# Softmax normalisation of 24 of 32 head groups on GpSimd instead of VectorE, with a new static order

## The chip, the cores and the metric

The kernel runs on one core of a Trainium2 chip. The metric is the device time of one launch in microseconds (us); lower is better. The engines are named as in the profile: PE (TensorE, matmuls), DVE (VectorE), ACT (ScalarE), POOL (GpSimd), SP (SyncE, which issues the DMAs).

## The reference

Two layers, each an attention block and an MLP block with a residual, on x of 2048 tokens by 640 in float32. The attention is local and dilated: each token looks at itself and at the seven tokens 2, 4, ... 14 before it; 32 heads of 20.

```python
def _A_ref(x, wqkv, wo):
    H = 32; Dh = D // H
    W, dil = 8, 2
    qkv = (x @ wqkv).reshape(B, S, 3, H, Dh)
    idx = pos[:, None] - (jnp.arange(W) * dil)[None, :]
    ...
    logits = jnp.einsum("bhsd,bhswd->bhsw", q, kg) * scale
    logits = jnp.where(mask, logits, -1e9)
    attn = softmax(logits, axis=-1)
    o = jnp.einsum("bhsw,bhswd->bhsd", attn, vg)
    return o.reshape(B, S, D) @ wo

def _B_ref(x, w1, b1, w2, b2):
    h = gelu(layernorm(x) @ w1 + b1)      # 640 -> 1536
    return h @ w2 + b2                    # 1536 -> 640

x = x + _A_ref(layernorm(x));  x = x + _B_ref(layernorm(x))
x = x + _A_ref(layernorm(x));  x = x + _B_ref(layernorm(x))
```

## The kernel before

The tokens are cut into four *units* of 512 (even and odd tokens apart, each in two halves), and with two layers there are eight unit passes n = 0 to 7; units 0 to 3 are layer one. In a unit each of 128 partitions holds four tokens. Every matrix product is computed in float16 in three passes over high and low halves, so each float32 operand is split first: ACT writes the high half, DVE the low one (L615 for normalised tokens, L435 for weights, L858 and L1076 for the MLP's hidden values).

A unit goes through these steps. Layernorm (for units 0 and 1 statistics by DVE, L561 to L563, and a power of -0.5 of one element on POOL, L566; for the others ACT sums and a power of two or one elements on POOL, L590). Products with wqkv on PE (L654; L661 for the very first tile, which is cut in three parts so that it can begin before the low halves are there), drained by ACT and spilled to DRAM. Then attention in four *head groups* of eight heads, G = 4n + g, all of it elementwise work: q times the eight windows of k (L741), the sum over the 20 channels that makes the logits (L745), for half of the units a mask (L750), maximum and difference (L753, L754), exp on ACT (L756), sum, reciprocal and product that normalise (L758, L759, L760), the product with v (L767) and three additions over the window (L775, L779). In units 0 to 2 a group's L741, L745 and L767 come in two halves of 2560 elements, from unit 3 on whole, 5120. The output is split (high half ACT, low half L788, on POOL for g = 0 to 2 and on DVE for g = 3), transposed by DMA (L799), multiplied by wo on PE (L810, eight blocks of fifteen matmuls in a unit) and added to x by DVE from PSUM (L816). Then the second layernorm and the MLP: first product L847, second L866 and L869, residuals L889; batches 5 to 7 go through a fast scheme with fewer columns (L1061 or L1024 for the first product, L1124 for the second, residuals L1143). POOL also adds the bias b2 to x (L624).

Nothing of this is scheduled by the hardware's own choice: every step is recorded with its needs, and three tables written into the file replay a schedule that a planner made earlier. ORDER lists all steps in the order in which they are issued, and so the order on each engine, which each works through in turn; PLACES gives the buffer of each tile; BESIDE names pairs, where the first step (on POOL) is given a wait for the second (on DVE), so that it begins with the DVE instruction that follows that one. In the kernel before, BESIDE ties 49 steps of L624 and L788 so. The attention's buffers set limits on the order: one for q and k, one for v, two for the products (both taken by a whole group), two for logits (`sm`).

At the start nine steps of eight matmuls on an identity (`warm`, L1153) keep PE busy until the first products; the normalised tokens of the first two tiles are transposed on PE (L489) and copied out by ACT (L497).

Of the kernel before, what the change touches and what calls it, by code (L numbers as in the profile page):

```python
# [261 lines left out]
def sliding_dilated_then_mlp_kernel(  # L262
# [87 lines left out]
    wo = sb.tile([P, 2, KD, D], HT, name="wo")  # L350
    b1 = sb.tile([P, NF], FT, name="b1")
    b2 = sb.tile([P, D], FT, name="b2")
    half = sb.tile([P, M], FT, name="half")
    junk = sb.tile([P, D], HT, name="junk")
    ident = sb.tile([P, P], HT, name="ident")
    bn = sb.tile([P, M, 14], FT, name="bn")
# [349 lines left out]
    def attention(G):  # L706
# [22 lines left out]
        def lgt():  # L729
            return lg().rearrange("p t w h -> p t h w")  # L730
# [428 lines left out]
    for _ in range(WARM):  # L1159
        warm([("sq", ("a", 0), 0)])  # L1160
# [74 lines left out]
```

## Time and profile before

| | |
|---|---|
| median of 3 runs | 1144.4 us (1144.36 to 1145.14) |
| the profiled execution's own time | 1144.26 us |
| its span in the trace | 1142.5 us |
| busy: PE, DVE, ACT, POOL | 1134.2, 1073.7, 552.5, 159.1 us |
| mean granted clock of PE | 0.998 |

The span runs from the first to the last instruction that the profiler shows; the execution's own time has 1.8 us around it. "Busy" is time in which at least one instruction of the engine runs. A group's row gives the source line, engine, operation, tiles written and read, shapes, how often, then busy time, mean duration in ns, and idle time before it with what ended that. PE's matmuls are pipelined, so a group's busy time divided by its count, and not its mean duration, is the pitch from one matmul to the next.

### The profile page before, as it was taken

Reading aid. Unit: us, or ns where it says so; the run is one execution under the profiler, and the core shown is the slowest. Engines: PE = TensorE matmul, PEld = TensorE weight load, DVE = VectorE, ACT = ScalarE, POOL = GpSimd, SP = SyncE. Lnnn points to the kernel's source line nnn. Section 1 sums busy time; section 2 is a strip of 40 time slices with the busy share of each in tenths; the row PEclk is TensorE's granted clock in tenths of the full one; section 3 lists DMA queues with packets and bytes.
Section 4 is the critical chain, followed back from the end, with each engine's and each line's share of the span. In section 5 each row is a group of like instructions: output and inputs, shape, how many; then the busy total and the mean of one; then the engine's idle time right before and its main releaser. Section 6 shows DMA issues by size and latency. Waiting matters only on the chain.

```text
span 1142.5 us, 17648 instructions
## 1 busy us (share of the span) xinstructions
PE 1134.2 (99%) x6932; PEld 647.0 (57%) x6932; DVE 1073.7 (94%) x1003; ACT 552.5 (48%) x977; POOL 159.1 (14%) x98
## 2 busy tenths in 40 slices
PE   8999999999999999999999999999999999999998
PEld 5444446577654565445555654556455546566886
DVE  8899999999999999999999999999999999988482
ACT  5476434545364438423645552355447542286360
POOL 2011110311111113100213011121211200300000
PEclk9999999999999999999999999999999999999999
DMA  9999999899976675956475866674598877788856
GB/s 295 324 311 277 278 331 279 262 266 308 240 198 196 216 192 125 253 182 188 155 216 188 179 188 188 213 190 133 164 267 275 258 209 221 211 218 225 251 152 189
DMA packets 259023, 257.38 MB, mean 225 GB/s; under 512 B 138540, under 2 KB 209532, under 8 KB 258940
## 3 DMA queue, kind: packets, MB, share of 16 engines
q1 hardware_dynamic: 258940, 256.26, 78.0%
q8 instruction: 54, 0.88, 0.3%
q14 instruction: 29, 0.24, 0.1%
HBM read 175.64 MB, written 48.71 MB: 196 GB/s over the span
## 4 chain that ended last, share of the span: by engine, by line
PE 99%; DVE 0%; DMA 0%; issue 0%
PE ps L654 34%; PE ps L847 17%; PE acc L866 14%; PE ps L810 11%; PE acc L1124 9%; PE ps L1061 7%; PE acc L869 4%; PE acc L1024 3%; PE ps L1024 1%; PE acc L1153 0%; DMA xf<-in_A_x_dram 0%; PE ps L661 0%; DVE bn L561 0%; PE acc L489 0%; DVE hl L615 0%; DVE bn L562 0%
## 5 line engine op out<-in xcount | busy, mean ns | idle before, releaser
L654 PE MATMUL ps<-wq,yT 128*128 128x480 f16 x1905 | 390.4, 366 | 0.0
L654 PEld LDWEIGHTS <-yT 128*128 128x128 f16 x1905 | 185.6, 98 | 197.0
L847 PE MATMUL ps<-yT,c 128*128 128x512 f16 (+1 forms) x1080 | 204.0, 344 | 0.0
L866 PE MATMUL acc<-c,act 128*128 128x512 f16 x720 | 203.4, 379 | 0.0
L741 DVE TENSOR_TENSOR pr<-qk 128x2560 f32<-128x2560 f32 (+1 forms) x44 | 179.6, 4088 | 0.7
L767 DVE TENSOR_TENSOR pr<-sm,v 128x2560 f32<-128x2560 f32 (+1 forms) x44 | 177.1, 4032 | 0.4
L745 DVE TENSOR_REDUCE sm<-pr 128x128 f32<-128x2560 f32 (+1 forms) x44 | 176.6, 4017 | 0.0
L847 PEld LDWEIGHTS <-c 128*128 128x128 f16 x1080 | 103.8, 98 | 87.4
L673 ACT ACTIVATE ev<-ps 128x480 f32<-128x480 f32 x128 | 70.7, 564 | 162.9 <-PE ps L654 155.5
L869 PE MATMUL acc<-c,act 128*128 128x128 f16 x720 | 148.2, 219 | 0.0
L775 DVE TENSOR_TENSOR pr<-pr 128x2560 f32<-128x2560 f32 (+2 forms) x88 | 143.8, 1645 | 0.2
L810 PE MATMUL ps<-wo,yT 128*128 128x320 f16 x960 | 134.7, 299 | 0.0
L866 PEld LDWEIGHTS <-act 128*128 128x128 f16 x720 | 70.3, 98 | 80.3 <-DVE act L858 0.2
L810 PEld LDWEIGHTS <-yT 128*128 128x128 f16 x960 | 93.0, 98 | 38.1
L590 POOL TENSOR_TENSOR ln<-ln,half 128x2 f32<-128x2 f32 (+1 forms) x30 | 48.6, 1621 | 408.9 <-ACT ln L587 408.9
L1124 PE MATMUL acc<-c,wq 128*128 128x320 f16 x630 | 92.9, 299 | 0.0
L853 ACT ACTIVATE act<-ps,b 128x512 f32<-128x512 f32 (+1 forms) x72 | 43.8, 613 | 93.1 <-PE ps L847 56.0
L624 POOL TENSOR_TENSOR xf<-xf,b 128x640 f32<-128x640 f32 x28 | 58.1, 2085 | 172.9 <-DVE xf L816 36.0
L788 POOL TENSOR_TENSOR ohl<-o,ohl 128x640 f16<-128x640 f32 x24 | 44.3, 1846 | 266.6 <-ACT ohl L786 118.7
L1061 PE MATMUL ps<-yT,c 128*128 128x512 f16 x360 | 78.7, 379 | 0.0
L1124 PEld LDWEIGHTS <-wq 128*128 128x128 f16 x630 | 61.6, 98 | 24.2
L571 ACT ACTIVATE junk<-xf 128x640 f16<-128x640 f32 x56 | 41.1, 733 | 66.8 <-DVE xf L816 54.8
(137 smaller groups left out, 1145.1 us busy)
## 6 DMA issues: line engine op xcount, KB each, us to landing
c<-mw SPq DMA_DIRECT2D x180, 320.0 KB, 4.0
spill<-ev SPq DMA_DIRECT2D x64, 480.0 KB, 5.6
qk<-spill SPq DMA_DIRECT2D x32, 880.0 KB, 5.4
v<-spill SPq DMA_DIRECT2D x32, 880.0 KB, 5.7
c<-msp SPq DMA_DIRECT2D x36, 320.0 KB, 3.6
qk<-spill SPq DMA_DIRECT2D x32, 320.0 KB, 4.8
c<-mw SPq DMA_DIRECT2D x54, 160.0 KB, 3.1
mw<-c SPq DMA_DIRECT2D x24, 320.0 KB, 5.6
```

What stands on the lines that cost most here:

```text
L654: nc.tensor.matmul(ps, transposed(yk)[:, a * KD + k, t * P:(t + 1) * P], wq[:, b, k, g], start=j == 0, stop=j == 3 * KD - 1)
L673: act(3 * GC, -400 + n, lambda i=i, pk=pk, ek=ek: nc.scalar.activation(tile_of(*ek)[:, :, i], tile_of(*pk)[:, :3 * GC].rearrange("p (a c) ...
L741: return nc.vector.tensor_mul(pr(pk), w[:, HALO + m + t0:HALO + m + t0 + TH, None, :].to_broadcast([P, TH, W, GC]), windows(w, t0, [GC, W] ...
L745: dve(E, G - 0.7, lambda pk=pk, t0=t0: nc.vector.tensor_reduce(lg(t0, t0 + TH).rearrange("p t w h -> p (t w h)"), pr(pk).rearrange("p t w ...
L767: return nc.vector.tensor_mul(pr(vk).rearrange("p t w (h d) -> p t (w h) d", d=DH), lg(t0, t0 + TH).rearrange("p t w h -> p t (w h)")[:, : ...
L775: dve(TH * w * GC, G - 0.9, lambda vk=vk, w=w: nc.vector.tensor_add(pr(vk)[:, :, 0:w], pr(vk)[:, :, 0:w], pr(vk)[:, :, w:2 * w]), need=[la ...
L810: nc.tensor.matmul(tile_of(*pk)[:, :D // 2], transposed(yk)[:, a * KD + k, t * P:(t + 1) * P], wo[:, b, k, c * D // 2:(c + 1) * D // 2], s ...
L847: nc.tensor.matmul(tile_of(*pk)[:, :nt], tile_of(*ck)[:, a, k * P:(k + 1) * P], transposed(yk)[:, c * KD + k, t0 * P:t1 * P], start=i == 0 ...
L866: nc.tensor.matmul(acc[i], w, tile_of(*wk)[:, c, :BANK], start=e == 0 and (a, c) == PASS[0], stop=end, skip_group_check=True)
L869: nc.tensor.matmul(acc[4][:, i * P:(i + 1) * P], w, tile_of(*wk)[:, c, BANK:], start=e == 0 and i == t0 and (a, c) == PASS[0], stop=end, s ...
L1061: nc.tensor.matmul(tile_of(*pk), tile_of(*ck)[:, a, k * P:(k + 1) * P], transposed(yk)[:, c * KD + k, :], start=i == 0, stop=i == 3 * KD - 1)
L1124: nc.tensor.matmul(acc[bank][:, :HD], tile_of(*hk)[half][:, a, slot, t * P:(t + 1) * P], load()[:, z, c], start=q in FIRST and i == 0 and ...
```

## The change

For the 24 groups with g = 0 to 2 the three DVE steps L758, L759 and L760 go. In their place POOL adds the exponentials in a tree (4, 2 and 1 window positions by eight heads by four tokens: 128, 64 and 32 elements), raises the 32 sums to the power of -1 and multiplies the 256 exponentials by the result; each of the five needs the one before. Each is tied by BESIDE so that the chain begins with the sum of logits (L745, now L760) of the next group. The groups with g = 3 stay as they were. A constant `minus` and a scratch tile `parts` are added; all groups share `parts`. The second token tile of the first products is cut in three parts too (`t in (0, 1)`), and the warming matmuls lose a need that only the planner used. The three tables are new throughout. Lines of the changed kernel lie some 14 to 31 further down.

```diff
@@ tables (all lines of ORDER and PLACES differ; of BESIDE the first) @@
-    278: 298, 302: 649, 326: 163, 395: 403, 400: 538, 405: 555, 410: 724, 497: 203, 520: 533, 543: 552, 607: 778, 612: 778, 617: 802, 622: 802,
+    269: 1, 270: 1, 271: 1, 272: 1, 273: 106, 283: 660, 295: 132, 296: 132, 297: 132, 298: 132, 299: 132, 309: 156, 321: 148, 322: 148, 323: 148,
@@ -351,6 +363,8 @@
     b1 = sb.tile([P, NF], FT, name="b1")
     b2 = sb.tile([P, D], FT, name="b2")
     half = sb.tile([P, M], FT, name="half")
+    minus = sb.tile([P, 1, 1], FT, name="minus")
+    parts = sb.tile([P, M * GH * W // 2], FT, name="parts")
     junk = sb.tile([P, D], HT, name="junk")
     ident = sb.tile([P, P], HT, name="ident")
     bn = sb.tile([P, M, 14], FT, name="bn")
@@ -394,6 +408,7 @@
         return nc.vector.memset(half, -0.5)
 
     dve(8, -900, constants, give=["half"])
+    dve(8, -100, lambda: nc.vector.memset(minus, -1.0), give=["minus"])
 
     def mask_index():
         nc.gpsimd.iota(mask, pattern=[[1, M], [1, W]], base=-HALO, channel_multiplier=M, allow_small_or_imprecise_dtypes=True)
@@ -655,7 +670,7 @@
                                              start=j == 0, stop=j == 3 * KD - 1)
                             j += 1
 
-                if n == 0 and g == 0 and t == 0:
+                if n == 0 and g == 0 and t in (0, 1):
                     def part(a, b, t=t, g=g, pk=pk):
                         for k in range(KD):
                             nc.tensor.matmul(tile_of(*pk)[:, :3 * GC], transposed(yk)[:, a * KD + k, t * P:(t + 1) * P], wq[:, b, k, g],
@@ -665,8 +680,8 @@
                     for a, c in ((0, 0), (1, 0), (0, 1)):
                         here = [("yT", ("a", n), t, a)] + [(("wq", "wqh")[1 - c], g, i) for i in range(3)]
                         mm(KD * 3 * GC, 5, -500, lambda a=a, c=c, part=part: part(a, c), need=here + last,
-                           give=[("qkvp", n, t, g) if c else ("qkvq", a)], use=[pk, yk])
-                        last = [("qkvq", a)]
+                           give=[("qkvp", n, t, g) if c else ("qkvq", t, a)], use=[pk, yk])
+                        last = [("qkvq", t, a)]
                 else:
                   mm(3 * KD * 3 * GC, 15, (-500 + n if n != NU else 24 + 11 * b) + 0.01 * k, product,
                    need=([("yT", ("a", n), t, a) for a in range(2)] if n == 0 and t not in (2, 3) else [("yT", ("a", n), t)]) + [("wq", g, i) for i in range(3)], give=[("qkvp", n, t, g)], use=[pk, yk])
@@ -755,10 +770,26 @@
             need=[("mx", G)], give=[("sub", G)], use=[sk])
         act(L, -450 + G, lambda: nc.scalar.activation(tile_of(*sk)[:, :L], tile_of(*sk)[:, :L], AF.Exp, scale=scale),
             need=[("sub", G)], give=[("e", G)], use=[sk], table="exp")
-        dve(L, G - 0.8, lambda: nc.vector.tensor_reduce(mx(1), lgt(), axis=AX.X, op=OP.add), need=[("e", G)], give=[("s", G)], use=[sk], more=0.19)
-        dve(8 * m * GH // 2, G - 0.8, lambda: nc.vector.reciprocal(mx(1), mx(1)), need=[("s", G)], give=[("rc", G)], use=[sk])
-        dve(L, G - 0.8, lambda: nc.vector.tensor_mul(lg(), lg(), mx(1)[:, :, None, :].to_broadcast([P, m, W, GH])),
-            need=[("rc", G)], give=[("at", G)], use=[sk])
+        if G in range(3, 32, 4):
+            dve(L, G - 0.8, lambda: nc.vector.tensor_reduce(mx(1), lgt(), axis=AX.X, op=OP.add), need=[("e", G)], give=[("s", G)], use=[sk], more=0.19)
+            dve(8 * m * GH // 2, G - 0.8, lambda: nc.vector.reciprocal(mx(1), mx(1)), need=[("s", G)], give=[("rc", G)], use=[sk])
+            dve(L, G - 0.8, lambda: nc.vector.tensor_mul(lg(), lg(), mx(1)[:, :, None, :].to_broadcast([P, m, W, GH])),
+                need=[("rc", G)], give=[("at", G)], use=[sk])
+        else:
+            after = ("lg", G + 1, 0 if (n + (g == NG - 1)) in WHOLE else m // EH - 1)
+            last = [("e", G)] + [("s", i) for i in range(G) if i not in range(3, 32, 4)][-1:]
+            for w in (4, 2, 1):
+                def add(w=w):
+                    part = parts.rearrange("p (t w h) -> p t w h", t=m, w=W // 2)
+                    src = lg() if w == W // 2 else part
+                    return nc.gpsimd.tensor_tensor(mx(1)[:, :, None, :] if w == 1 else part[:, :, :w], src[:, :, :w], src[:, :, w:2 * w], op=OP.add)
+
+                laid(m * w * GH, -700 + G, add, lambda ready, when, k=after: k in when, need=last, give=[("s", G) if w == 1 else ("sp", G, w)], use=[sk])
+                last = [("s", G) if w == 1 else ("sp", G, w)]
+            laid(m * GH, -700 + G, lambda: nc.gpsimd.tensor_tensor(mx(1), mx(1), minus.to_broadcast([P, m, GH]), op=OP.pow),
+                 lambda ready, when, k=after: k in when, need=[*last, "minus"], give=[("rc", G)], use=[sk])
+            laid(L, -700 + G, lambda: nc.gpsimd.tensor_tensor(lg(), lg(), mx(1)[:, :, None, :].to_broadcast([P, m, W, GH]), op=OP.mult),
+                 lambda ready, when, k=after: k in when, need=[("rc", G)], give=[("at", G)], use=[sk])
         for a in range(NE):
             t0 = a * TH
             vk = products(a, 1)
@@ -1157,7 +1188,7 @@
     load_x(0, -1000)
     prep_q(0, -990)
     for _ in range(WARM):
-        warm([("sq", ("a", 0), 0)])
+        warm([])
     layernorm(0, -500, ("yT", ("a", 0)), False)
     for g in range(1, NG):
         prep_q(g, -480 + g)
```

**DVE and POOL at group 2** (unit 0, halves of 2560). In both kernels `sm_85` holds the logits of group 2 here and `sm_86` those of group 3. DVE before, from the second product of q and k of group 3 to the products with v of group 2:

```order
L741 TENSOR_TENSOR pr<-qk_68 128x2560
L758 TENSOR_REDUCE sm_85<-sm_85 128x32
L745 TENSOR_REDUCE sm_86<-pr 128x128
L435 SCALAR_TENSOR_TENSOR c_77<-act,c_77 128x640
L745 TENSOR_REDUCE sm_86<-pr 128x128
L759 RECIPROCAL sm_85<-sm_85 128x32
L615 TENSOR_TENSOR hl_83<-y_80,hl_83 128x640
L760 TENSOR_TENSOR sm_85<-sm_85 128x256
L435 SCALAR_TENSOR_TENSOR c_79<-act,c_79 128x640
L767 TENSOR_TENSOR pr<-sm_85,v_69 128x2560 x2
```

DVE after, the same stretch:

```order
L756 TENSOR_TENSOR pr<-qk_68 128x2560 x2
L768 TENSOR_REDUCE sm_85<-sm_85 128x32
L769 TENSOR_TENSOR sm_85<-sm_85 128x256
L450 SCALAR_TENSOR_TENSOR c_77<-act,c_77 128x640
L760 TENSOR_REDUCE sm_86<-pr 128x128
L450 SCALAR_TENSOR_TENSOR c_78<-act,c_78 128x640
L760 TENSOR_REDUCE sm_86<-pr 128x128
L798 TENSOR_TENSOR pr<-sm_85,v_69 128x2560 x2
```

POOL after, beside it, between the low halves of groups 1 and 2:

```order
L819 TENSOR_TENSOR ohl_73<-o_84,ohl_73 128x4x160
L785 TENSOR_TENSOR parts<-sm_85 128x128
L785 TENSOR_TENSOR parts<-parts 128x4x16
L785 TENSOR_TENSOR sm_85<-parts 128x32
L789 TENSOR_TENSOR sm_85<-sm_85,minus 128x32
L791 TENSOR_TENSOR sm_85<-sm_85 128x256
L819 TENSOR_TENSOR ohl_73<-o_84,ohl_73 128x4x160
```

The normalisation of group 2 left DVE; POOL's five steps are tied to the L450 on c_78, and between that and the product with v that needs them stands one L760 of 2560 elements. Before, POOL had only L788 and L590 steps in this stretch.

**SP before the last unit's transposes.** The transposes L799 (now L830) of unit 7 feed its L810; the loads of L1055 (now L1086) bring the blocks of w1 for the first product of batch 6 (L1061). Before:

```order
L1055 DMA c_74<-mw_110 128x1280
L1055 DMA c_76<-mw_116 128x1280
L940 DMA v_69<-in_B_w_dram 128x5x128
L1055 DMA c_75<-mw_111 128x1280
L1112 DMA c_77<-mw_130 128x2x320
L940 DMA v_69<-in_B_w_dram 128x5x128
L1055 DMA c_74<-mw_117 128x1280
L940 DMA pr<-in_B_w_dram 128x5x128 x3
L1055 DMA c_76<-mw_112 128x1280
L799 DMA_TRANSPOSE yT_72<-ohl_73 128x10x128
L940 DMA pr<-in_B_w_dram 128x5x128
L799 DMA_TRANSPOSE yT_72<-ohl_73 128x10x128 x3
```

After:

```order
L1143 DMA c_74<-mw_133 128x2x320
L1143 DMA c_74<-mw_132 128x2x320
L1086 DMA c_76<-mw_116 128x1280
L971 DMA v_69<-in_B_w_dram 128x5x128 x2
L971 DMA pr<-in_B_w_dram 128x5x128 x3
L830 DMA_TRANSPOSE yT_72<-ohl_73 128x10x128 x3
L1086 DMA c_74<-mw_111 128x1280
L830 DMA_TRANSPOSE yT_72<-ohl_73 128x10x128
L1086 DMA c_75<-mw_110 128x1280
```

On PE nine of the twelve blocks of that first product stood ahead of the first L810 of unit 7, and one does now; one L810 block of unit 7 stands ahead of the one that was first.

**ACT at the start.** `wq<-pr` are the high halves of the first weight blocks, `yT<-acc` the copies of the first two tiles' transposes. Before:

```order
L613 ACTIVATE hl_82<-y_80 128x640
L434 ACTIVATE wq<-pr 128x5x160 x3
L613 ACTIVATE hl_82<-y_80 128x640
L613 ACTIVATE hl_83<-y_81 128x640
L497 ACTIVATE yT_70<-acc_94 128x5x128
L497 ACTIVATE yT_70<-acc_95 128x5x128
```

After:

```order
L628 ACTIVATE hl_82<-y_80 128x640
L449 ACTIVATE wq<-pr 128x5x160 x2
L512 ACTIVATE yT_70<-acc_94 128x5x128
L628 ACTIVATE hl_83<-y_81 128x640
L628 ACTIVATE hl_82<-y_80 128x640
L449 ACTIVATE wq<-pr 128x5x160
L512 ACTIVATE yT_70<-acc_95 128x5x128
```

The third weight block comes later on ACT, as its load does on SP, where a block of the second head group now stands between the second and the third. On PE all nine warming steps stand ahead of the first transposes, where four did.

More of the change, by code (lines that the diff above doesn't have):

```diff
@@ L71 @@
 ORDER = """
[111 rows of a table removed]
[113 rows of a table added]
 """
 PLACES = """
-000000000110000110101032320001111220230203102102132000110303222011120003200121102220011202120002200001001000110100001011000001110010221012110201100111
-010110011012022101012122011201022001001000001100010010010000011001020120120002110100121210001102101202010121202111002200000100100001100100001100001101
-000102112021120011001010100011011212000121202000200112000010010000011010000100100001101012020101220011001102011101001211202021210101021210201000100100
-000110100001001000011010210201210002110001100011001102201102001222010101221020001001000001101000010010000110100012200121000111100111111000020011202120
@@ L190 @@
-101022100011200010010000011010000100100001101011220021000101111002010110011021210100220112001211201000100100000110100001001000011010220010221200212301
-132012012112000002021102002111002021102002111102020102012111002021102012111000002021102002111102020102012111002021102002111102000102112111100000020201
-020121100020211020022111010201020122111010201020022101000000101010201221100101110200221110102010201221210101010201211200000002011102002112102010102012
-112002011102112112002001102202110100000020101222120100010111222020101010101222120100010111222020001102210011102220011232100041212150001100022002100120
@@ L194 @@
-02110022100020211101021212100023211114020205100102002011020020110221100220200011010110000022220200311010140000025200211000022010010220110220
+000000000110000110100231010203111221201223021021000113100223010223202311000121012210011200102211200001001000011100001000010011010012001201211210011001
+111001001000222111002120212122001000001000001101000010000100110001021012010012001011020211000110211021102201001201122000000110000011010000100001000110
+010022110211120010110010100110022011210022101010222111000010010000011010000100100001101010120210221010001102111001001121102110210002120212100000100100
@@ new lines @@
+000110100001001000011010212010121012101110000011010011201002100212000101222010001001000001101000010010000110100020101121000110110101110011021212000012
+201211022111100010010000011010000100100001101012011210201100100112011100011200122110220100112102011000100100000110100001001000011010212212101201202321
+301012012012000002001112202010102020112102010102020112112010002021112112010000002021112102010102020112112010002021112102010102020112012012000000020011
+121120120020111120020121020101120120120020111120020111000000200011221201100200111220201110200011221201100200111201201200000002011102012212001011102002
@@ L195 @@
+211101020102002111102020102012111000000020211020021111020201022121100020011022021111020001022121102000211112000221112031200242111052001100002210000122
+10012210101200010201021112200023111204020115200002001122100001221001221000000021020110201022100200321000140201025100021000211000022110022110
 """
 BESIDE = {
[4 rows of a table removed]
[14 rows of a table added]
 }
```

240 rows, old and new, of tables (BESIDE, ORDER) are left out of this document.

## The prediction

> **What bounds the kernel now.** I read the shares of busy time, the chain that ended last, what TensorE waited for, and then stretches of the span. Page, parts 1 and 4:
>
> ```profile
> PE 1134.2 (99%) x6932; PEld 647.0 (57%) x6932; DVE 1073.7 (94%) x1003; ACT 552.5 (48%) x977; POOL 159.1 (14%) x98
> PE 99%; DVE 0%; DMA 0%; issue 0%
> ```
>
> TensorE's waits, all of them (us in total, times, longest), and busy time by stretch (length, then PE, PEld, DVE, ACT, POOL, granted clock, DMA):
>
> ```profile
> PE acc L489 <- ACT hl L613: 2.8, 1, 2.8
> PE acc L1153 <- POOL ident L406: 1.4, 1, 1.4
> PE acc L489 <- DVE hl L615: 0.7, 1, 0.7
> ...
> 7.80:13.36 5.56, 4.82 (x55) 4.65 (x56) 5.18 (x9) 4.70 (x7) 1.21 (x1) 0.69 1.11 343
> 13.36:1139.08 1125.72, 1125.72 (x6848) 638.97 (x6845) 1064.24 (x982) 545.78 (x969) 155.74 (x89) 1.00 0.78 225
> 1139.08:1142.50 3.42, 0.00 (x0) 0.00 (x0) 0.49 (x1) 0.00 (x0) 0.00 (x0) 0.95 0.34 120
> ```
>
> From the first product at 13.36 to 1139.08 TensorE is busy for 1125.72 of 1125.72 us at clock 1.00. The change takes no matmul away. So time can be won only before 13.36 or in the 3.4 us tail, and time saved on DVE is worth nothing by itself. It can be lost anywhere: DVE is busy for 1064 of those 1126 us, and what makes TensorE wait shifts everything behind it.
>
> **What leaves DVE.** Groups by form (busy, mean ns, idle before):
>
> ```profile
> L745 DVE TENSOR_REDUCE sm<-pr 128x256 f32<-128x5120 f32 x20 | 109.4, 5470 | 0.0
> L745 DVE TENSOR_REDUCE sm<-pr 128x128 f32<-128x2560 f32 x24 | 67.2, 2806 | 0.0
> L758 DVE TENSOR_REDUCE sm<-sm 128x32 f32<-128x256 f32 x32 | 19.5, 609 | 0.0
> L760 DVE TENSOR_TENSOR sm<-sm 128x256 f32<-128x256 f32 x32 | 13.3, 416 | 0.2
> L759 DVE RECIPROCAL sm<-sm 128x32 f32<-128x32 f32 x32 | 11.1, 346 | 0.2
> ```
>
> Each moved group loses 0.609 + 0.346 + 0.416 = 1.37 us of DVE; 24 of them 32.9 us. In its place the products with v (L767, now L798) wait for GpSimd. The two L745 rows are the cover: GpSimd's chain is tied to start beside one such sum, 2.81 us long for units 0 to 2 (nine moved groups), 5.47 us from unit 3 on (fifteen).
>
> **What GpSimd's chain costs.** Three additions (128, 64, 32 elements), a power of 32, a product of 256. GpSimd's timeline at quiet places, then beside two-input DVE work with DVE's own rows (start, us), and the group that L858 belongs to:
>
> ```profile
> 5.06 0.15 DVE L563 TENSOR_SCALAR bn<-bn 128x1 f32<-128x1 f32 x1
> ...
> 5.30 0.57 POOL L566 TENSOR_TENSOR bn<-bn,half 128x1 f32<-128x1 f32 x1 [4.01 <-DVE bn L563]
> ...
> 30.59 0.55 POOL L566 TENSOR_TENSOR bn<-bn,half 128x1 f32<-128x1 f32 x1 [4.02 <-DVE bn L563]
> 668.81 0.69 POOL L590 TENSOR_TENSOR ln<-ln,half 128x2 f32<-128x2 f32 x1 [2.22 <-ACT ln L587]
> 472.77 1.55 POOL L624 TENSOR_TENSOR xf<-xf,b 128x640 f32<-128x640 f32 x1 [14.65 <-DVE hl L615]
> ...
> 598.54 8.68 POOL L624 TENSOR_TENSOR xf<-xf,b 128x640 f32<-128x640 f32 x2 [19.18 <-DVE sm L760]
> ...
> 598.38 5.48 DVE L741 TENSOR_TENSOR pr<-qk 128x5120 f32<-128x5120 f32 x1
> 603.78 2.03 DVE L858 TENSOR_TENSOR act<-act 128x512 f16<-128x512 f32 x1
> ...
> L858 DVE TENSOR_TENSOR act<-act 128x512 f16<-128x512 f32 x48 | 35.3, 737 | 0.6 <-ACT act L856 0.6
> ```
>
> The addition of 640 elements at 472.77 ran beside an L745: 1.55 us, some 2.3 ns an element over a tenth. By it the three additions are about 0.40, 0.25 and 0.18 us, the product 0.68; five hand-overs at some 0.09 (DVE's L563 ends at 5.06 + 0.15, GpSimd's first power starts at 5.30) make it 2.0 us without the power.
>
> The power of 32 elements is the unknown. The trace has it for one element (0.55) and two (0.69). Upper end: each element 0.14 to 0.15 more, 0.40 + 32 x 0.15 = 5.2 us. Lower end: as an addition of 32, 0.18 us. I take 5.2: the nearest rows are powers, and their second element cost some sixty times an addition's. The chain is then 7.2 us (with the lower end 2.2). The Trainium skill, page "GPSIMD Engine Reference", section 3.1, gives elementwise work on GpSimd about 2.6 cycles an element; if the power obeyed that estimate the end would be the first rival's, 1144.3, and the power rows speak against it.
>
> **What DVE then waits.** Under a 2.81 us sum: 7.2 - 2.8 = 4.4 us, for eight of nine early groups (the product with v follows at once, or after two-input work); group 9 has two sums before it and waits about 3.2. That is 38.4. Under a 5.47 us sum: 1.7 us, or 25 for fifteen, of which sums over the logits and residuals read from PSUM, where such stand between the sum and the product with v (units 5 to 7), hide some 3: 22. Together 60. It matters whether two-input DVE work between (L858, L615) can run under the power. At 598.54 GpSimd's first L624 got through only with DVE's L741, and then L858, 0.74 us by its group, took 2.03 beside the second. So each holds the other off; I let nothing of that kind hide the wait. If it could, the 60 would be 47.
>
> **What of it reaches TensorE.** The place to look is L810 of each unit, which needs the last group's output, split by DVE (L788) and transposed by DMA. Timeline at units 2 and 7 (DVE, then PE), the transposes (us to landing), busy time up to there, and two PE groups of the page:
>
> ```profile
> 403.61 0.82 DVE L788 TENSOR_TENSOR ohl<-o,ohl 128x640 f16<-128x640 f32 x1
> 414.06 0.38 PE L866 MATMUL acc<-c,act 128*128 128x512 f16 x1
> ...
> 414.33 0.38 PE L866 MATMUL acc<-c,act 128*128 128x512 f16 x1
> ...
> 414.60 1.11 PE L810 MATMUL ps<-wo,yT 128*128 128x320 f16 x7
> 999.42 0.82 DVE L788 TENSOR_TENSOR ohl<-o,ohl 128x640 f16<-128x640 f32 x1
> 1009.07 1.11 PE L810 MATMUL ps<-wo,yT 128*128 128x320 f16 x7
> ...
> yT<-ohl SPq DMA_TRANSPOSE x32, 4.3
> ...
> 0.00:40.00 40.00, 35.07 (x223) 21.03 (x224) 31.69 (x63) 23.83 (x35) 8.71 (x16) 0.96 1.00 298
> 40.00:404.40 364.40, 364.40 (x2187) 204.07 (x2186) 361.18 (x327) 180.64 (x349) 49.57 (x27) 1.00 0.91 265
> 0.00:1000.20 1000.20, 995.27 (x5898) 545.93 (x5899) 980.03 (x828) 482.72 (x860) 156.84 (x96) 1.00 0.79 228
> ...
> L810 PE MATMUL ps<-wo,yT 128*128 128x320 f16 x960 | 134.7, 299 | 0.0
> L1061 PE MATMUL ps<-yT,c 128*128 128x512 f16 x360 | 78.7, 379 | 0.0
> ```
>
> In both places TensorE came to L810 without a wait, some 9 to 10 us after DVE was done with L788, of which the transposes need about 4.5 (4.3 and a hand-over).
>
> Unit 2: DVE has worked 31.69 + 361.18 = 392.9 us by 404.4. In the new order 8.8 less stands ahead (nine groups, 12.3, against 3.5 of other pieces moved up): 384.1, and 8.3 of the first 40 us are waits that stay. TensorE comes to L810 with 3.2 us more ahead (one block of fifteen L810 matmuls, 15 x 134.7/960 = 2.1, and four L866 and L869 pairs, one each 0.27 by the starts at 414.06 and 414.33): 417.8, less 4.5 for a transpose. Allowance 417.8 - 4.5 - 384.1 - 8.3 = 20.9; waits 38.4; TensorE loses 17.5.
>
> Unit 7: 980.0 - 36.0 (32.9 and 3.1 of pieces moved behind) = 944.0. TensorE comes earlier: eight blocks of fifteen L1061 matmuls of batch 6, 8 x 15 x 78.7/360 = 26.2 us, now stand behind unit 7's first L810, one L810 block of 2.1 ahead: 1009.1 - 24.1 = 985.0. Allowance 985.0 - 4.5 - 944.0 - 8.3 = 28.2; waits 60; loss 31.8. This contains unit 2's loss, since a shift of TensorE serves all that follows. With 47 for 60 it is 18.8.
>
> GpSimd is in order: behind each chain stand L590 (ScalarE's normalisation waits), L624 and L788 (the transposes wait), some 5 us late and then beside L767, where they are held as at 598.54. I price that at nothing, since no row shows which would come last; it is in the upper end.
>
> **The start.** TensorE, then ScalarE (start, us):
>
> ```profile
> 9.49 3.76 PE L1153 MATMUL acc<-ident 128*128 128x128 f16 x40
> ...
> 13.36 1.18 PE L661 MATMUL ps<-wq,yT 128*128 128x480 f16 x5
> 14.37 0.44 PE L489 MATMUL acc<-ident,hl 128*128 128x128 f16 x5
> 14.65 2.19 PE L661 MATMUL ps<-wq,yT 128*128 128x480 f16 x10
> ...
> 9.13 0.87 ACT L434 ACTIVATE wq<-pr 128x800 f16<-128x800 f32 x1 [0.44 <-DMA pr<-in_A_wqkv_dram]
> 10.40 0.87 ACT L434 ACTIVATE wq<-pr 128x800 f16<-128x800 f32 x1 [0.40 <-DMA pr<-in_A_wqkv_dram]
> ```
>
> All 72 warming matmuls now stand first and the first products come behind both token tiles' transposes. The third weight block is fourth in SP's queue, one spacing later: 10.40 + 1.27 + 0.87 gives a first product near 12.6. Against 13.36 and the 0.28 us of transposes at 14.37 that is 1.0 us won. Against it: TensorE now idles between 9 and 12, as it idled before 7.79, after which the clock averaged 0.69 over 5.56 us, 1.7 us lost, then on filler alone. On products that loss would count. So -1.0 to +0.7; I take 0. The Trainium skill, "TensorE: Matmul & The Clock Gate", Part 1, says the clock halves after an idle window of a free-running 3.4 us; by it the loss depends on the phase of each run, and the start would be at the +0.7 end, the sum 1176.8; the 0.69 agrees with it. Nothing changes in the tail.
>
> **Sum.** 31.8 + 0 on the profiled 1144.26 us (span 1142.5 and 1.8 around it; 0.1 under the median of 1144.4): 1176. The same sums for other powers: with 4.0 us the early groups wait 3.2 and the late ones 0.5, together 36, loss 8, end 1152; with 5.7 us 4.9 and 2.2, together 73, loss 45, end 1189.
>
> **Rivals.** *The power is cheap (not slower).* Anything up to about 3.1 us leaves the early waits (power + 2.0 - 2.8 each, times nine) within unit 2's allowance of 20.9, and the later ones nil. Then only the start moves: 1143.2 to 1145.0. For it: two short powers are a thin basis for 32. *Cheap, but held off.* If the ties fail and chains run beside L741 or L767, each can lose a DVE instruction of 5.5 us, as at 598.54; six such by unit 7 exceed its allowance (33 against 28.2): about 1149. Against it: sums stand behind nearly every tie. *Faster.* The start would have to give 2.3 us, a first product at 11.3, before the third block has landed at 11.7; only a luckier DMA order or tail could.
>
> **Chances.** Expensive power 0.56, held off 0.07, cheap 0.32, faster 0.05. Faster, same, slower by 0.2% (2.3 us, about what this kernel's runs can tell): 0.05, 0.32, 0.63. Range 1143 to 1187: it takes in the cheap case and most of the expensive one, whose own range is 1152 to 1189.
>
> **What would show it.** The L789 power near 5 us; DVE idle before L798, released by GpSimd, 40 to 60 us in all; TensorE waiting at L810 of units 1, 2 and 7. A power under 3 us, or none of DVE's waits reaching TensorE, makes this wrong.

## Result and the profile after

| | before | after |
|---|---|---|
| median of 4 runs each, same chip | 1144.77 us (1144.36 to 1145.19) | 1223.32 us (1222.03 to 1225.72) |
| span of the profiled execution | 1142.5 us | 1220.3 us |
| mean granted clock of PE | 0.998 | 0.985 |

The ratio is 1.0687, with a 95% interval of 1.0674 to 1.0699: slower by 79 us. The forecast was 1176, at most 1187; its direction was right, its size not.

Part 1 of the page after, then the groups by form (busy, mean ns, idle before and what ended it) of the products with v, where L767 stood, and of the power:

```profile
PE 1155.0 (95%) x6932; PEld 650.9 (53%) x6932; DVE 1051.2 (86%) x932; ACT 553.9 (45%) x979; POOL 320.8 (26%) x218
...
L798 DVE TENSOR_TENSOR pr<-sm,v 128x5120 f32<-128x5120 f32 x20 | 114.3, 5717 | 42.7 <-POOL sm L791 42.7
L798 DVE TENSOR_TENSOR pr<-sm,v 128x2560 f32<-128x2560 f32 x24 | 68.6, 2876 | 38.9 <-POOL sm L791 38.9
L789 POOL TENSOR_TENSOR sm<-sm,minus 128x32 f32<-128x32 f32 x24 | 130.1, 5422 | 1.8
```

The power takes 5.42 us, and VectorE waits 42.7 + 38.9 = 81.6 us ahead of its products with v. TensorE, which hardly waited before, now waits in small pieces (us in total, times, longest):

```profile
PE ps L841 <- DVE xf L847: 22.2, 8, 5.0
PE acc L897 <- DVE act L889: 9.5, 8, 2.4
PE ps L669 <- ACT ev L688: 9.4, 8, 2.3
```

One such place in the timeline: GpSimd, VectorE, TensorE (start, us, and in brackets the wait), and the stretches (busy PE, PEld, DVE, ACT, POOL, granted clock):

```profile
194.03 5.42 POOL L789 TENSOR_TENSOR sm<-sm,minus 128x32 f32<-128x32 f32 x1
...
192.59 2.81 DVE L760 TENSOR_REDUCE sm<-pr 128x128 f32<-128x2560 f32 x1
200.28 2.83 DVE L798 TENSOR_TENSOR pr<-sm,v 128x2560 f32<-128x2560 f32 x1 [4.88 <-POOL sm L791]
...
211.02 0.88 DVE L847 SCALAR_TENSOR_TENSOR xf<-ps,xf 128x320 f32<-128x320 f32 x2
...
200.26 6.28 PE L841 MATMUL ps<-wo,yT 128*128 128x320 f16 x45
211.56 10.67 PE L841 MATMUL ps<-wo,yT 128*128 128x320 f16 x57 [5.02 <-DVE xf L847]
...
206.50:211.50 5.00, 0.04 (x1) 0.00 (x0) 4.97 (x7) 0.00 (x0) 0.00 (x0) 0.89 0.21 79
211.50:218.30 6.80, 6.74 (x30) 3.92 (x30) 6.48 (x7) 3.94 (x10) 1.02 (x1) 0.58 0.36 116
```

The product with v starts 4.88 us after VectorE went idle. TensorE's own L841 starts without a wait at 200.26, but its fourth block needs a PSUM bank that the residual L847 frees, and L847 stands behind L798 on VectorE's queue. TensorE stops for 5.0 us and then runs at a granted clock of 0.58.

The split of the whole loss: TensorE's idle time went from 8.3 (1142.5 - 1134.2) to 65.3 us (1220.3 - 1155.0), and its busy time grew by 20.8 us with the same 6932 matmuls; together 77.8, the difference of the spans (1220.3 - 1142.5). This says where TensorE lost time, not yet what set it. That came out of the experiments below, by an account of VectorE's time up to the last head group. From here on line numbers are those of the kernel after: L810 is now the last addition of a head group's products with v, the context sum (L779 before), and the product with wo, which was L810 before, is L841. The next rows are VectorE's busy time from 0 to the end of the last split of a context sum (L819), in after and in two experiments, norm_vector and pow_one (length, then busy, clock, DMA share, GB/s):

```profile
0.00:1055.43 1055.43, 953.31 (x751) 0.98 0.73 213
...
0.00:998.60 998.60, 978.24 (x823) 1.00 0.77 225
...
0.00:980.34 980.34, 949.42 (x751) 1.00 0.78 229
```

After: 1055.43 - 953.31 - 81.6 of waits for GpSimd = 20.5 us of other idle time. norm_vector, which never waits for GpSimd: 20.4. Before, by the prediction's row: 1000.20 - 980.03 = 20.2. So VectorE was nearly full before as well; before_fill below shows how much of its 20 us could still be used. And what follows is fixed. The last context sum L810 in after, with the residual L1174 behind it and TensorE's wait for that; then L810 in pow_one, with the split L819 and TensorE's first projection L841 of the last unit:

```profile
1052.97 0.83 DVE L810 TENSOR_TENSOR o<-pr 128x640 f32<-128x640 f32 x1
1053.72 0.48 DVE L1174 SCALAR_TENSOR_TENSOR xf<-acc,xf 128x320 f32<-128x320 f32 x1
...
1054.25 0.57 PE L1155 MATMUL acc<-c,wq 128*128 128x320 f16 x3 [0.53 <-DVE xf L1174]
...
977.89 0.83 DVE L810 TENSOR_TENSOR o<-pr 128x640 f32<-128x640 f32 x1
...
979.52 0.82 DVE L819 TENSOR_TENSOR ohl<-o,ohl 128x640 f16<-128x640 f32 x1 [0.40 <-ACT ohl L817]
...
985.66 10.35 PE L841 MATMUL ps<-wo,yT 128*128 128x320 f16 x75
```

From the end of L810 to the end of the span it is 1220.3 - 1053.8 = 166.5 and 1145.2 - 978.7 = 166.5. The link is L1174: it stands right behind L810 on VectorE's queue, and in every kernel of the new order TensorE's L1155 waits 0.5 us for it. From the end of L810 on TensorE is busy for 162.4 of the 166.5 us, in after, norm_vector and pow_one alike. The kernel before has no such wait. The table has the account for every kernel that ran (in the two of the old order the context sum is L779 or L782):

| kernel | median us | last L810 ends | VectorE busy till then | waits for the chain's product L791 | other idle | from there to the end |
|---|---|---|---|---|---|---|
| before | 1144.8 | 997.2 | 977.1 | 0 | 20.1 | 145.3 |
| pow_one | 1146.2 | 978.7 | 948.2 | 0.2 | 30.3 | 166.5 |
| recip_vector | 1160.3 | 992.3 | 959.2 | 12.7 | 20.4 | 166.4 |
| norm_vector | 1164.6 | 996.9 | 976.9 | 0 | 20.0 | 166.4 |
| pow_half | 1166.5 | 998.4 | 951.1 | 25.2 | 22.1 | 166.4 |
| before_fill | 1168.6 | 1021.4 | 1008.6 | 0 | 12.8 | 144.9 |
| early_only | 1180.7 | 1011.3 | 948.0 | 38.9 | 24.4 | 166.5 |
| late_only | 1187.7 | 1019.9 | 952.3 | 42.5 | 25.1 | 166.5 |
| whole_untied | 1199.0 | 1030.4 | 964.9 | 38.5 | 27.0 | 166.4 |
| untied | 1199.8 | 1031.2 | 954.8 | 57.7 | 18.7 | 166.4 |
| fill_vector | 1214.0 | 1045.2 | 1025.8 | 0 | 19.4 | 166.5 |
| after | 1223.3 | 1053.8 | 952.1 | 81.6 | 20.1 | 166.5 |
| chain_whole | 1228.4 | 1059.7 | 967.0 | 65.8 | 26.9 | 166.5 |

Other idle time holds VectorE's waits for GpSimd's other work: 4.4 us in chain_whole and 3.5 in whole_untied (L920, for a late residual L639), 0.4 in the two kernels of the old order. That the columns add up to the span is arithmetic. What the runs show is that two of them hardly move: in the new order the end comes 166.4 to 166.5 us after L810, and the other idle time is 18.7 to 27.0 us (25.1 without the late residuals), so that VectorE's work and its waits set the end. Only pow_one has more idle time, 30.3: there TensorE sets the pace, and about 10 us of VectorE are to spare.

### The profile page after: what moved, and what is told of

It is laid out like the page before. It is cut to its first block, busy times and chain, and to the rows that moved or that the text cites. A ratio compares the mean times of both kernels' runs of the same rounds, so it can differ in the third digit from the quotient of the medians.

```text
span 1220.3 us, 17686 instructions
## 1 busy us (share of the span) xinstructions
PE 1155.0 (95%) x6932; PEld 650.9 (53%) x6932; DVE 1051.2 (86%) x932; ACT 553.9 (45%) x979; POOL 320.8 (26%) x218
## 5 line engine op out<-in xcount | busy, mean ns | idle before, releaser
L798 DVE TENSOR_TENSOR pr<-sm,v 128x2560 f32<-128x2560 f32 (+1 forms) x44 | 182.9, 4167 | 81.6 <-POOL sm L791 81.6
L897 PE MATMUL acc<-c,act 128*128 128x512 f16 x720 | 206.7, 382 | 12.3 <-DVE act L889 9.5
L756 DVE TENSOR_TENSOR pr<-qk 128x2560 f32<-128x2560 f32 (+1 forms) x44 | 177.0, 4031 | 3.3 <-DMA qk<-spill 2.7
L760 DVE TENSOR_REDUCE sm<-pr 128x128 f32<-128x2560 f32 (+1 forms) x44 | 176.8, 4021 | 0.1
L841 PE MATMUL ps<-wo,yT 128*128 128x320 f16 x960 | 144.1, 310 | 24.2 <-DVE xf L847 22.2
L806 DVE TENSOR_TENSOR pr<-pr 128x2560 f32<-128x2560 f32 (+2 forms) x88 | 144.0, 1647 | 0.5
L841 PEld LDWEIGHTS <-yT 128*128 128x128 f16 x960 | 95.7, 101 | 68.1 <-issue 25.9
L789 POOL TENSOR_TENSOR sm<-sm,minus 128x32 f32<-128x32 f32 x24 | 130.1, 5422 | 1.8
L897 PEld LDWEIGHTS <-act 128*128 128x128 f16 x720 | 70.7, 99 | 92.1 <-DVE act L889 12.1
L605 POOL TENSOR_TENSOR ln<-ln,half 128x2 f32<-128x2 f32 (+1 forms) x30 | 55.0, 1835 | 183.8 <-ACT ln L602 183.8
L1155 PE MATMUL acc<-c,wq 128*128 128x320 f16 x630 | 93.6, 299 | 1.5 <-DVE wq L1107 1.0
L639 POOL TENSOR_TENSOR xf<-xf,b 128x640 f32<-128x640 f32 x28 | 53.5, 1917 | 145.5 <-DVE ohl L819 56.6
L785 POOL TENSOR_TENSOR parts<-sm 128x128 f32<-128x128 f32 x24 | 10.9, 456 | 258.3 <-DVE act L889 86.9
```

The source lines that it names most:

```text
L756: return nc.vector.tensor_mul(pr(pk), w[:, HALO + m + t0:HALO + m + t0 + TH, None, :].to_broadcast([P, TH, W, GC]), windows(w, t0, [GC, W] ...
L760: dve(E, G - 0.7, lambda pk=pk, t0=t0: nc.vector.tensor_reduce(lg(t0, t0 + TH).rearrange("p t w h -> p (t w h)"), pr(pk).rearrange("p t w ...
L789: laid(m * GH, -700 + G, lambda: nc.gpsimd.tensor_tensor(mx(1), mx(1), minus.to_broadcast([P, m, GH]), op=OP.pow), lambda ready, when, k=a ...
L798: return nc.vector.tensor_mul(pr(vk).rearrange("p t w (h d) -> p t (w h) d", d=DH), lg(t0, t0 + TH).rearrange("p t w h -> p t (w h)")[:, : ...
L806: dve(TH * w * GC, G - 0.9, lambda vk=vk, w=w: nc.vector.tensor_add(pr(vk)[:, :, 0:w], pr(vk)[:, :, 0:w], pr(vk)[:, :, w:2 * w]), need=[la ...
L841: nc.tensor.matmul(tile_of(*pk)[:, :D // 2], transposed(yk)[:, a * KD + k, t * P:(t + 1) * P], wo[:, b, k, c * D // 2:(c + 1) * D // 2], s ...
```

## Experiments

All are built on the kernel after, but before_fill, which is built on the kernel before. Ratios are to the kernel before on the same chip, with 95% intervals. In kernels with added lines the line numbers below the edit are one to three higher.

**pow_one: the power of one element.** Only one of the 32 sums is inverted.

```diff
-            laid(m * GH, ..., lambda: nc.gpsimd.tensor_tensor(mx(1), mx(1), minus.to_broadcast([P, m, GH]), op=OP.pow),
+            laid(m * GH, ..., lambda: nc.gpsimd.tensor_tensor(mx(1)[:, :1, :1], mx(1)[:, :1, :1], minus, op=OP.pow),
```

> The power on GpSimd is taken of one element in 32 (31 reciprocals are left out); order, ties, sums and product stay. Queue theory (the power makes the chain outlast the sum it runs beside, and what stands behind the waiting product on VectorE's queue holds TensorE at once): the power falls from 5.42 to about 0.55 us, the chain from 7.5 to about 2.7, under the sum's 2.81 or 5.48; VectorE's waits for it fall from 81.6 us to under 15, TensorE's idle time from 65 to 8 to 20 us, and the time to 1143 to 1160. Order theory (the new order and its ties cost by themselves, the power little): 1185 to 1215.

Measured: 1146.2 us, ratio 1.0012 (1.0002 to 1.0021).

```profile
PE 1134.9 (99%) x6932; PEld 646.0 (56%) x6932; DVE 1047.2 (91%) x932; ACT 556.1 (49%) x979; POOL 186.3 (16%) x218
...
L789 POOL TENSOR_TENSOR sm<-sm,minus 128x1 f32<-128x1 f32 x24 | 13.3, 554 | 1.8
L791 POOL TENSOR_TENSOR sm<-sm 128x256 f32<-128x256 f32 x24 | 17.4, 727 | 1.7
```

The power's length makes the loss: 77 of the 79 us go with it, at the same order and ties. And even with nearly the whole normalisation off VectorE the kernel is not faster than before; TensorE is again at 99%.

**norm_vector: the new order, the normalisation on VectorE.**

```diff
-   nc.gpsimd.tensor_tensor(...)   # three additions, power, product
+   nc.vector.tensor_reduce(mx(1), lgt(), axis=AX.X, op=OP.add)
+   nc.vector.reciprocal(mx(1), mx(1))
+   nc.vector.tensor_mul(lg(), lg(), mx(1)[:, :, None, :].to_broadcast([P, m, W, GH]))
```

> The changed order and ties, but sum, reciprocal and product are VectorE's again, as 0.60, 0.25 and 0.56 us in the places where GpSimd's had stood. Queue theory: 24 x 1.4 = 34 us come back to VectorE, which had them before; no wait for GpSimd is left, 1143 to 1152. Order theory: 1185 to 1215 as with the short power.

Measured: 1164.6 us, ratio 1.0170 (1.0153 to 1.0187): neither. VectorE does what it did before, in 0.60 + 0.35 + 0.42 us a group, and yet 18 us more than pow_one. Part 4 of its page, the chain that ended last, which was 99% TensorE before:

```profile
PE 53%; DVE 35%; issue 9%; DMA 2%; ACT 1%; SPq 1%; DVEq 0%; ACTq 0%
```

So the order does cost something, and by VectorE's time: it keeps 166.4 us for after the last L810 where the old one kept 145.3, and is level with the old one only if VectorE is done some 20 us earlier.

**pow_half: the power of 16 elements.** The slices are mx(1)[:, :m // 2] in place of [:, :1, :1].

> The power on 16 of 32 elements (half the reciprocals are left out). By 0.55 us for one element and 5.42 for 32 the power takes about 2.9 us and the chain 5.0. Queue theory: early waits 4.9 - 2.5 = 2.4 us in nine groups, about 22; the late ones, beside a sum of 5.48, only where other GpSimd work stands within the chain, about 10; 30 us in all, passed on with the slower clock at 0.96 us for each: about 1172 (1160 to 1180). The prediction's allowances (21 us before the first, 28 before the second TensorE wait) would leave 9 x 2.4 = 22 us at nothing: 1143 to 1148.

Measured: 1166.5 us, ratio 1.0189 (1.0174 to 1.0204), within the first theory's range, and far from the 1143 to 1148 that the prediction's allowances would give.

```profile
L789 POOL TENSOR_TENSOR sm<-sm,minus 128x16 f32<-128x16 f32 x24 | 69.7, 2904 | 1.8
...
DVE pr L798 <- POOL sm L791: 25.2, 17, 2.4
```

0.554, 2.904 and 5.422 us for 1, 16 and 32 elements: 0.157 us for each further one, in both halves.

**fill_vector: the delay without the power.**

```diff
             def pv(t0=t0, vk=vk, a=a):
+                if a == 0 and G % 4 != 3:
+                    nc.vector.tensor_reduce(fill, half[:, None, :].to_broadcast([P, 800, M]), axis=AX.XY, op=OP.add)
                 return nc.vector.tensor_mul(
```

(and the short power of pow_one).

> The power of one element, so that GpSimd is early, but VectorE makes a sum of 3200 elements that nobody reads (about 3.4 us) ahead of the first product with v in each of the 24 groups: 82 us of VectorE's time where the changed kernel waited 81.6. Queue theory (VectorE's delay alone is the cost): 1205 to 1235. Rival (GpSimd's own queue, layernorm powers and residuals behind the long power, is what holds TensorE): 1150 to 1180.

Measured: 1214.0 us, ratio 1.0602 (1.0586 to 1.0618).

```profile
L800 DVE TENSOR_REDUCE fill<-half 128x1 f32<-128x3200 f32 x24 | 83.4, 3475 | 0.0
...
PE ps L844 <- DVE xf L850: 22.2, 7, 5.0
```

83 us of useless work on VectorE cost 68 us over pow_one, with the same 22.2 us of TensorE waiting for the residuals' banks. GpSimd's late layernorm powers and residuals aren't needed to explain the loss.

**early_only and late_only: the whole power in nine groups, or in the fifteen others.** Edit: the operands of pow_one or those of the kernel after, by `G < 12` and `G >= 12`.

> The whole power in the nine groups before group 12, one element of 32 in the fifteen after (31 reciprocals are left out there). Their waits were 39 of the 81.6 us. Pace theory (VectorE is full up to the last group's sum, L810, and what follows takes the same 166.5 us in all kernels of this order, so that every wait beyond some 15 us of slack moves the end): last L810 near 1003 to 1010 us, 1170 to 1180. The prediction's allowances would give 17.5 for these groups: 1162 to 1164.

> The mirror of early_only: one element in the first nine groups, the whole power in the fifteen late ones, whose waits were 43 us. Pace theory: 43 less the slack of 15, and a slower clock where TensorE stops: 1170 to 1185; with early_only's gain over 1146 it adds up to about the whole kernel's 77, or 15 less. The prediction's allowances: 43 less 28, then 1158 to 1162; with 22 us of waits, as it took them, 1145.

Measured: 1180.7 (ratio 1.0314, 1.0299 to 1.0330) and 1187.7 us (1.0374, 1.0356 to 1.0391), 34.5 and 41.5 over pow_one, together 76.0; the whole power costs 77.1. VectorE's waits:

```profile
DVE pr L799 <- POOL sm L792: 38.9, 9, 4.9
...
DVE pr L799 <- POOL sm L792: 42.5, 15, 4.6
```

Both halves pass on nearly all they wait and they add up; little of the early groups' waits is absorbed later. Both came a little above the upper end of what the pace theory gave (1180 and 1185): I had granted them 15 us of slack, and it is 10 at most. By the table's other idle time some 6 and 5 us of it were used.

**before_fill: is VectorE's slack in the old order any larger?** The fill of 1240 elements, [P, 310, M], in the kernel before.

> The kernel before, and VectorE makes a sum of 1240 elements that nobody reads (about 1.4 us) ahead of the first product with v in the same 24 groups, 33 us in all. Pace theory (VectorE was as full as TensorE before, 199.6, 198.4 and 197.5 of each 200 us between 200 and 800): 1160 to 1180. The prediction's reading (TensorE bounds, VectorE's queue has 21 to 28 us to spare): 1145 to 1152.

Measured: 1168.6 us, ratio 1.0209 (1.0193 to 1.0224). The last context sum came 24 us later for 32 us of work. The kernel before had 7 us to spare (20.1 us of idle time, of which 12.8 stay).

**untied: the chains start when they can.** The 120 entries of the chains' steps are taken out of BESIDE; every engine has the same instructions in the same order.

> The same instructions in the same order on every engine; only the 120 ties that hold the chain's steps on GpSimd back to a VectorE step are dropped, so that a chain starts when the exponential is done. That was 0.1 to 22.7 us before the chain's start, in the median 4.8. Pace theory: of each wait min(wait, that gap) goes, which leaves about 22 of 81.6 us: 1155 to 1170, like the half power. Rival (GpSimd beside VectorE's two-input products holds itself or them up, as the ties would avoid): L791, L785 or L756 clearly longer, waits of 50 us and more, 1185 and above.

Measured: 1199.8 us, ratio 1.0479 (1.0463 to 1.0495): 23 us less than after, but the rival was right. GpSimd's groups, the waits, and one chain with VectorE beside it:

```profile
L785 POOL TENSOR_TENSOR parts<-sm 128x128 f32<-128x128 f32 x24 | 35.3, 1472 | 151.6 <-ACT sm L771 151.6
...
DVE pr L798 <- POOL sm L791: 57.7, 17, 4.7
...
244.82 6.66 POOL L785 TENSOR_TENSOR parts<-sm 128x128 f32<-128x128 f32 x1 [12.05 <-ACT sm L771]
...
252.29 5.44 POOL L789 TENSOR_TENSOR sm<-sm,minus 128x32 f32<-128x32 f32 x1
...
244.20 2.82 DVE L756 TENSOR_TENSOR pr<-qk 128x2560 f32<-128x2560 f32 x1
246.94 0.82 DVE L630 TENSOR_TENSOR hl<-y,hl 128x640 f16<-128x640 f32 x1
247.67 2.82 DVE L756 TENSOR_TENSOR pr<-qk 128x2560 f32<-128x2560 f32 x1
250.41 0.76 DVE L889 TENSOR_TENSOR act<-act 128x256 f16<-128x256 f32 x2
251.08 2.82 DVE L760 TENSOR_REDUCE sm<-pr 128x128 f32<-128x2560 f32 x1
```

An addition that took 0.456 us in its place takes 6.66: it gets nowhere beside five two-input instructions and ends 0.4 us into the sum. So here the early start brought nothing before the next sum began. The Trainium skill, page "SBUF — State Buffer", section "Who interferes with whom", says that a VectorE instruction with two inputs from SBUF contends with a GpSimd instruction that reads SBUF, for a pair of ports that works as an exclusive lock; the addition of 6.66 us agrees. The power is held up less: most powers stood beside sums in this run too, and the five that took longer, 5.88 to 6.54 us, had two-input work under way as they began. One of them then ran beside L806, L450, L810 and L756 and still took only 5.88.

**chain_whole: GpSimd's other work out of the chains.** In ORDER the 14 steps of other work inside eleven chains (seven L819 and seven L639, not the numbers that the expectation has) go behind the chain's product.

> Only GpSimd's order is changed: the 14 steps of other work (nine low halves L819, seven residuals L639 less two that are not alone) that stand within a chain go behind its product. Eleven waits get shorter by 1.2 to 2.9 us, 17 of 81.6 in all. Pace theory: 1223 - 0.9 x 17, about 1208 (1203 to 1213). Rival (the power alone sets the waits, other work within a chain is a trifle, or what is moved back is then late itself): 1220 to 1226.

Measured: 1228.4 us, ratio 1.0735 (1.0719 to 1.0751): slower than after by 5, where 15 us less were expected, and above the rival's 1226 too. VectorE's waits fell nearly as expected, by 15.8 us of 17, and came back as work. The waits, the group to set beside after's mean of 5717 ns, and one place in both engines' timelines, of chain_whole:

```profile
DVE pr L798 <- POOL sm L791: 65.8, 22, 4.9
DVE xf L920 <- POOL xf L639: 4.4, 1, 4.4
...
L798 DVE TENSOR_TENSOR pr<-sm,v 128x5120 f32<-128x5120 f32 x20 | 125.5, 6274 | 26.9 <-POOL sm L791 26.8
...
722.44 1.41 POOL L819 TENSOR_TENSOR ohl<-o,ohl 128x640 f16<-128x640 f32 x1
723.79 5.96 POOL L605 TENSOR_TENSOR ln<-ln,half 128x2 f32<-128x2 f32 x1
...
722.52 6.67 DVE L798 TENSOR_TENSOR pr<-sm,v 128x5120 f32<-128x5120 f32 x1 [1.63 <-POOL sm L791]
```

L819, now started just ahead of L798, makes it 6.67 us instead of 5.49 as at the same group in after, and L605 then takes 5.96 us beside L798. Over the twenty large L798 this is 125.5 - 114.3 = 11.2 us, and a residual that comes late costs VectorE 4.4 more.

**whole_untied: both edits.**

> chain_whole and untied together, still the whole power of 32. If the two add: 57.7 us of waits less some 15, about 1185 (1175 to 1192). Rival (a chain that starts early only waits longer beside the two-input products, so the ties were worth nothing and nothing more is to be had): 1195 to 1205.

Measured: 1199.0 us, ratio 1.0481 (1.0463 to 1.0498), as untied alone; the rival was right. Against untied the waits for L791 went from 57.7 to 38.5, VectorE's work up to the last L810 from 954.8 to 964.9 and its other idle time from 18.7 to 27.0, of which 3.5 are a wait for a late residual.

**recip_vector: only the reciprocal goes back to VectorE.**

```diff
-   nc.gpsimd.tensor_tensor(mx(1), mx(1), minus.to_broadcast([P, m, GH]), op=OP.pow)
+   nc.vector.reciprocal(mx(1), mx(1))
```

> After's order and ties; the sum and the product stay GpSimd's, the reciprocal is VectorE's (0.35 us, 24 times, in the place of the power, behind the next group's sum). VectorE then waits for the product alone, 0.73 us and two hand-offs, about 0.9 each: 8 + 22 = 30 us on VectorE. Pace theory, by norm_vector (33 us: 1164.6) and pow_half (25 us: 1166.5): 1158 to 1170. Rival (only the 5.42 us power does harm, a wait under 1 us is hidden): 1145 to 1150.

Measured: 1160.3 us, ratio 1.0139 (1.0124 to 1.0155). VectorE has 11.0 us more work than in pow_one and 12.7 of waits (up to 0.8 each); 14 of these 24 us reach the end. It is the best of the kernels in the new order that normalise in full, and no gain on before. In pow_one, with 31 of 32 reciprocals left out, TensorE was busy for 99% and the time 1146.2, so another way to normalise in this order had hardly anything to win; none was tried.

## Why the prediction was right or wrong

- *Removed from VectorE, 24 x 1.37 = 32.9 us.* A little too much: norm_vector and pow_one differ by just these instructions, and by 976.9 - 948.2 = 28.7 us of busy time. Neighbours overlap in the trace (above, L630 starts at 246.94, where L756 ends at 244.20 + 2.82 = 247.02), so a sum of durations is more than the time they hold the engine.
- *The power, 5.2 us (bounds 0.18 and 5.2).* Right, if a little above the upper bound: 5.42. The rows of one and two elements (0.55, 0.69) gave 0.14 an element, the runs 0.157. The rule of the Trainium skill, page "GPSIMD Engine Reference", section 3.1, of some 2.6 cycles an element does not hold for this operation: 0.157 us an element is some fifty times what an element of the product costs (0.727 us for 256).
- *VectorE's waits, 60 us.* Mis-sized: 81.6. The nine early groups were right, 38.4 forecast and 38.9 measured. The fifteen late ones were 22 against 42.7. Of that 15.8 us is GpSimd's other work within the chains, by chain_whole (81.6 - 65.8): at L639 and L819 the chain is 8.7 to 10.4 us long instead of 7.5. I had counted such steps only behind a chain. Of the other 5 us the power's extra 0.2 makes 3 (15 x 0.2); the rest was not traced further.
- *The allowances of 20.9 and 28.2 us.* This is the step whose working failed, beside the waits that were sized too small above. TensorE came to unit 7's first projection when I said: 985.66 in pow_one, 985.0 forecast. But VectorE was done with the split at 980.34, not at 944.0 + 8.3 = 952.3. Its work ahead was 949.4 us, 5.4 more than I had summed (4.2 of it by the overstated removal); and its waits that stay are some 20 us (20.4 in norm_vector), not the 8.3 of the first 40 us. The prediction's own row showed 20.2 us of idle time, 980.03 busy of 1000.20, but not how much of it stays: in the old order before_fill has 12.8 left. Put in, 28.2 - 5.4 - 12.1 (20.4 - 8.3) leaves 10.7 us, and about 10 is what pow_one has. Loss then: 81.6 of waits and 3.9 of VectorE work longer than in pow_one (952.1 - 948.2), less 10, is 75.5; between the two spans it is 75.1. This is the table's account again, not a further test. Against the 31.8 that I forecast, 21.6 us are missing in the waits (81.6 - 60), 17.5 in the allowance (28.2 - 10.7) and 3.9 in VectorE's work. With only the waits put right the sum would have given 1198, with only the allowance 1194.
- *Checks at the first L810 (now L841) of units 1, 2 and 7.* Wrong place. None of TensorE's waits in after is for a transpose. It mostly waits for banks and operands that L847 and L889 give, which stand behind the waiting product on VectorE's queue, and for ScalarE's copies; in the last unit it waits for L1174 ahead of L841. The size was wrong with the place: early_only lost 34.5 us, where the step for unit 2 gave 17.5.
- *GpSimd's late L590 and L624 (now L605, L639), priced at nothing.* Nearly right for those behind a chain: fill_vector, with GpSimd early, still loses 68 of the 77 us. They are not free, though: where they run beside L798 it takes up to 6.82 us instead of 5.49, and the twenty large L798 take 114.3 us in after against 110.6 in pow_one, which is nearly all of the 3.9 above. Those within the chains cost more, the 15.8 us of waits.
- *"What bounds the kernel now": TensorE alone.* Half the truth. Both were nearly full up to the last head group: of before_fill's 31.5 us of added VectorE work only about 7 were absorbed.
- *The start, -1.0 to +0.7, taken as 0.* Within that. The first product came at 12.30 (12.6 forecast, 13.36 before), and then ran at a low clock, as the row and the stretch of after show:

```profile
12.30 7.92 PE L676 MATMUL ps<-wq,yT 128*128 128x480 f16 x30
...
12.00:16.00 4.00, 3.93 (x15) 1.57 (x12) 3.93 (x9) 3.66 (x6) 1.22 (x1) 0.57 1.46 331
```

  Thirty products in 7.92 us are 0.264 each; before, ten took 2.19. So 30 x 0.045 = 1.35 us are lost, against 13.36 - 12.30 + 0.28 = 1.34 won. The rule that the clock halves after an idle window of about 3.4 us (the Trainium skill, "TensorE: Matmul & The Clock Gate", Part 1) agrees with 0.58 behind the 5 us stop at 206.5. It fits the 0.57 here and the prediction's 0.69 less plainly, since TensorE's longest pauses ahead of them were 1.6 us (9.34 to 10.92) and 2.8.
- *The rivals.* "The power is cheap" came close for a power of 0.55 us: 1143.2 to 1145.0 forecast, 1146.2 in pow_one. Its bound of 3.1 us was wrong with the allowances: the power of 2.9 us in pow_half costs 20 us more than that.

## What to carry to other kernels

One engine at 99% does not mean that the next one has slack: take the second engine's idle time up to its last step that others need, strike what stays in any case, and only what is left can absorb a wait. A run with useless work on that engine, as before_fill, measures it. Work taken off one engine must come back sooner than the cover lasts, and that holds for the helper's whole in-order queue, with what else stands inside the chain. When two engines exclude each other, moving a step out of a wait can turn the wait into longer instructions.

## What was not expected of the hardware

- GpSimd's power is linear in its elements at 0.157 us each (0.554, 2.904 and 5.422 us for 1, 16 and 32 in each of 128 partitions).
- A GpSimd addition of 128 elements took 6.66 us instead of 0.456 beside VectorE's two-input instructions, and a VectorE product 6.67 instead of 5.49 when a GpSimd subtraction had started 0.08 us ahead of it. The power of 32 took at most 6.54 in any of these runs.
- TensorE's 20.8 us of longer busy time seem to add nothing of their own here: after at a granted clock of 0.985, fill_vector at 0.988 and norm_vector at 0.997 all have some 20 us of other idle time on VectorE (20.1, 19.4 and 20.0). No run changed the clock alone.
